# Small VectorE operations, a table built on TensorE instead of by transfers, a later square root and a tail in four parts: one change to a two-branch sequence kernel

## The chip, the cores and the metric

One core of one Trainium2 chip. The span, which the profile's views use, runs from the first to the last instruction and is some 1.8 us shorter than the time.

## The reference, cut to what matters

The input is 2048 tokens of 640 channels. Four residual layers follow one another, A, B, A, B, each behind a layer norm:

```python
x = x + _A_ref(_layernorm(x), Lambda, B, C, log_dt, Dskip)   # complex linear recurrence over the tokens
x = x + _B_ref(_layernorm(x), k, v, shift_k, ssm_k, ssm_D)   # q * (long convolution of k_shift*v + ...)
x = x + _A_ref(...)                                          # the same weights again
x = x + _B_ref(...)

# in _A_ref, per channel p of 640:
Lam_bar = exp(dt * Lam);  B_bar = ((Lam_bar - 1) / Lam)[:, None] * Bmat     # the factor here is "f"
h = Lam_bar * h + B_bar u_t;  y_t = 2 Re(C h) + x * Dskip
# in _B_ref, which does not depend on x except through q:
Y = irfft(rfft(kv, 2S) * rfft(ssm_k, 2S))[:S] + kv * ssm_D;  return q * Y
```

## The kernel before

Every piece of work is a task with a name, an engine, buffers and a wished time; a list scheduler puts the tasks into one order per engine when the kernel is built. Engines execute their own list strictly in that order. So a change of one task's cost or place shifts hundreds of others, and a diff of the code shows less than half of what changes.

The names that matter: `kv_` is the product k_shift*v (five blocks of 128 channels; its `ds` are diagonals that GpSimd builds), `yq0` to `yq4` are the five passes that compute Y (KA, KB and VA, VB transform forward, `pw` multiplies, IB and IA transform back), `a_` are the tables and weights of the A layers, `A1c0` is layer A the first time on chunk 0 of four, and `B2c3` the last B layer on the last chunk. An ending `m` or `mm` is TensorE's part, `e` or `ev` the evacuation of a PSUM tile by ScalarE or VectorE. There are four PSUM tiles of 1024 columns, and TensorE waits when none is free.

The inverse tables of the Y passes are DMA transposes of the forward ones:

```python
for a, b in (("Ci", "Cf"), ("Si", "Sf")):
    def e_tr(_, a=a, b=b):
        nc.sync.dma_start_transpose(out=T[a].get()[:], in_=T[b].get().rearrange("p q k -> p (q k)"))
    t_tr.append(S.add(f"yt_{a}", "sp", 3.5, sins, e_tr, xt=3.5, uses=[T[a], T[b]]))
```

The factor f is 25 operations on 128x5 elements (cut to its first lines):

```python
v.tensor_tensor(den[:], lre, lre, ALU.mult)
v.tensor_tensor(t2[:], lim, lim, ALU.mult)
v.tensor_tensor(den[:], den[:], t2[:], ALU.add)
nc.vector.reciprocal(inv[:], den[:])
# ... 21 more
```

The sine block of ScalarE fills the phase table of layer A, and the roots of the first layer norm (`A1c*_ln_sd`) have no tie to it:

```python
nc.scalar.activation(aw["tab"][:, 2], st["r"], ACT.Sin, scale=-2.0 * PI_LO)
nc.scalar.activation(ab, st["r"], ACT.Abs)
nc.scalar.activation(aw["tab"][:, 1], ab, ACT.Sin, bias=consts["half_pi"][:, 0:1], scale=-2.0 * PI_LO)
for j in range(NJ):
    nc.scalar.activation(aw["rtab"][:, j, :], st["it"], ACT.Identity, scale=0.0, bias=st["r2"][:, j:j + 1])
```

In the last chunk each quarter q takes two fused operations on VectorE, (x - mean) * Y and then times rstd plus x, and two stores follow.

Of the kernel before, what the change touches and what calls it, by code (L numbers as in the profile page):

```python
# [9 lines left out]
ALU = mybir.AluOpType  # L10
# [7 lines left out]
P = 128  # L18
L = 2048
D = 640  # L20
# [32 lines left out]
    "warm": -5, "yt_io0": 2.55, "yt_ph0": 4.27, "yt_sin0": 5.89, "yt_neg0": 9.88, "yt_io6": 132.6, "yt_ph6": 8.2, "yt_sin6": 9.91, "yt_neg6": 13.01,  # L53
    "yt_io12": 8.8, "yt_ph12": 11.54, "yt_sin12": 13.59, "yt_neg12": 16.53, "yt_Ci": 21.14, "yt_Si": 22.8, "yt_nsi": 30.27, "yt_f0": 1.22, "yt_f2": 6.07,
    "yt_f3": 8.4, "yt_f4": 9.65, "yt_h0": 0.07, "yt_h1": 0.97, "yt_h2": 5.13, "yt_h3": 9.63, "kv_dsl": 1.97, "kv_kd": 2.73, "kv_k0": 13.36, "kv_k1":
    14.32, "kv_k2": 14.97, "kv_d0": 5.67, "kv_d1": 6.57, "kv_d2": 10.23, "kv_ds0": 10.65, "kv_lk0": -0, "kv_lv0": 9.8, "kv_mm0:0": 12.25, "kv_ev0:0":
    15.4, "kv_mm0:1": 15.02, "kv_ev0:1": 17.2, "kv_st0": 21.1, "kv_ds1": 13.44, "kv_lk1": 12.55, "kv_lv1": 15, "kv_mm1:0": 21.79, "kv_ev1:0": 25.02,
    "kv_mm1:1": 20.06, "kv_ev1:1": 22.17, "kv_st1": 32.7, "kv_ds2": 18.01, "kv_lk2": 35.6, "kv_lv2": 40.3, "kv_mm2:0": 48.16, "kv_ev2:0": 52.03,
    "kv_mm2:1": 40.92, "kv_ev2:1": 50.79, "kv_st2": 54.8, "kv_ds3": 30.92, "kv_lk3": 47.3, "kv_lv3": 43.8, "kv_mm3:0": 54.17, "kv_ev3:0": 56.25,
    "kv_mm3:1": 57.88, "kv_ev3:1": 59.99, "kv_st3": 76.1, "kv_ds4": 55.32, "kv_lk4": 68.7, "kv_lv4": 72.6, "kv_mm4:0": 78.97, "kv_ev4:0": 81.57,  # L60
    "kv_mm4:1": 72.36, "kv_ev4:1": 77.61, "kv_st4": 85.5, "a_pl": 0.17, "a_p0": 11.24, "a_p1": 13.98, "a_p2": 14.63, "a_p3": 15.78, "a_p4": 18.43, "a_p5":
    20.56, "a_p6": 23.36, "a_lamd": 23.86, "a_f": 28.37, "a_dd": 16.07, "a_ldB0": 2.4, "a_ldB1": 7.4, "a_wl00:0": 34.4, "a_wl00:1": 31.5, "a_wc00:0":
    37.93, "a_wm00:0": 39.1, "a_wc00:1": 40.53, "a_wm00:1": 40.04, "a_wl01:0": 40.21, "a_wl01:1": 37.9, "a_wc01:0": 42.58, "a_wm01:0": 49.98, "a_wc01:1":
    51.1, "a_wm01:1": 53.25, "a_wl02:0": 46.1, "a_wl02:1": 42.6, "a_wc02:0": 48.69, "a_wm02:0": 54.03, "a_wc02:1": 55.37, "a_wm02:1": 58.88, "a_wl03:0":
    71.4, "a_wl03:1": 56.5, "a_wc03:0": 74.94, "a_wm03:0": 75.97, "a_wc03:1": 76.97, "a_wm03:1": 79.87, "a_wl04:0": 65.2, "a_wl04:1": 74.9, "a_wc04:0":
    78.59, "a_wm04:0": 80.65, "a_wc04:1": 81.65, "a_wm04:1": 82.89, "a_b00:0": 9.82, "a_b0e0:0": (10.51, 0), "a_b00:1": 8.06, "a_b0e0:1": (9.33, 3),
    "a_b00:2": 11.53, "a_b0e0:2": (13.01, 1.5), "a_b00:3": 10.63, "a_b0e0:3": (12.42, -1), "a_b00:4": 7.7, "a_b0e0:4": (8.75, 3), "a_b01:0": 49.89,
    "a_b0e1:0": (50.52, 3), "a_b01:1": 14.62, "a_b0e1:1": (17.28, 0.8), "a_b01:2": 23.8, "a_b0e1:2": (24.94, 3), "a_b01:3": 18.33, "a_b0e1:3": (19.59,
    -1), "a_b01:4": 23.52, "a_b0e1:4": (24.36, 1.5), "a_b10:0": 33.92, "a_b1e0:0": (35, 3), "a_b10:1": 32.55, "a_b1e0:1": (33.68, 0), "a_b10:2": 25.31,
    "a_b1e0:2": (26.42, -1), "a_b10:3": 29.77, "a_b1e0:3": (31.02, 0), "a_b10:4": 26.8, "a_b1e0:4": (28.17, 3), "a_b11:0": 42.65, "a_b1e1:0": (43.58, -1),  # L70
    "a_b11:1": 28.31, "a_b1e1:1": (29.65, -1), "a_b11:2": 34.63, "a_b1e1:2": (35.54, -1), "a_b11:3": 46.77, "a_b1e1:3": (48.11, 99), "a_b11:4": 30.56,
    "a_b1e1:4": (31.47, -1), "a_gm0": 84.5, "a_ge0": (87.86, -1), "a_gm1": 87.84, "a_ge1": 90.96, "a_gm2": 104.18, "a_ge2": (107.4, 0), "a_gm3": 98.47,
    "a_ge3": (115.43, 1.5), "a_gm4": 92.78, "a_ge4": 96.07, "a_wl10:0": 97.9, "a_wl10:1": 89.8, "a_wc10:0": 115.48, "a_wm10:0": 107.45, "a_wc10:1":
    111.58, "a_wm10:1": 112.92, "a_wl11:0": 101.84, "a_wl11:1": 103.04, "a_wc11:0": 106.68, "a_wm11:0": 109.36, "a_wc11:1": 121.12, "a_wm11:1": 122.95,
    "a_wl12:0": 116.24, "a_wl12:1": 117.44, "a_wc12:0": 121.91, "a_wm12:0": 132.45, "a_wc12:1": 135.94, "a_wm12:1": 138.06, "a_wl13:0": 131.59,
    "a_wl13:1": 130.39, "a_wc13:0": 137.56, "a_wm13:0": 138.85, "a_wc13:1": 139.99, "a_wm13:1": 141.05, "a_wl14:0": 144.12, "a_wl14:1": 142.92,
    "a_wc14:0": 148.92, "a_wm14:0": 150.68, "a_wc14:1": 153.82, "a_wm14:1": 157.45, "a_ti": 20.17, "a_ta": 22.96, "a_t0": 26.17, "a_t1": 122.82, "a_t2":
    131.25, "yq0_kl": 4.8, "yq0_ka": 15.17, "yq0_KA:m0": 16.75, "yq0_KA:e0": (18.76, -1), "yq0_KA:m1": 19.31, "yq0_KA:e1": 20.32, "yq0_KA:m2": 17.03,
    "yq0_KA:e2": (17.86, -1), "yq0_KA:m3": 18.61, "yq0_KA:e3": (19.66, 99), "yq0_KB:m0": 25.89, "yq0_KB:e0": (27.01, 99), "yq0_KB:m1": 27.38, "yq0_KB:e1":
    (28.75, 0.8), "yq0_KB:m2": 24.08, "yq0_KB:e2": (25.52, 1.5), "yq0_KB:m3": 28.87, "yq0_KB:e3": (30.31, 0), "yq0_KB:m4": 26.57, "yq0_KB:e4": 27.91,  # L80
    "yq0_vl": 26.3, "yq0_VA:m0": 31.92, "yq0_VA:e0": (32.55, 0), "yq0_VA:m1": 31.61, "yq0_VA:e1": (32.24, 6), "yq0_VA:m2": 32.27, "yq0_VA:e2": (33.15,
    0.8), "yq0_VA:m3": 33.47, "yq0_VA:e3": (34.1, 99), "yq0_VB:m0": 35.91, "yq0_VB:e0": 36.98, "yq0_VB:m1": 37.48, "yq0_VB:e1": (38.73, 99), "yq0_VB:m2":
    36.58, "yq0_VB:e2": (37.97, 0), "yq0_VB:m3": 38.79, "yq0_VB:e3": (41.58, 0), "yq0_VB:m4": 40.18, "yq0_VB:e4": (39.51, 1.5), "yq1_kl": 28.99, "yq1_ka":
    34.59, "yq1_KA:m0": 39.9, "yq1_KA:e0": (41.76, 1.5), "yq1_KA:m1": 35.29, "yq1_KA:e1": (35.98, 6), "yq1_KA:m2": 35.57, "yq1_KA:e2": 36.58, "yq1_KA:m3":
    38.6, "yq1_KA:e3": (39.71, 0.8), "yq1_KB:m0": 43.29, "yq1_KB:e0": (44.32, 3), "yq1_KB:m1": 45.76, "yq1_KB:e1": (47.02, 0), "yq1_KB:m2": 44.86,
    "yq1_KB:e2": 46.12, "yq1_KB:m3": 43.97, "yq1_KB:e3": 45.22, "yq1_KB:m4": 47.51, "yq1_KB:e4": 49.78, "yq0_pw": 42.46, "yq0_IB:m0": 52.34, "yq0_IB:e0":
    53.78, "yq0_IB:m1": 51.44, "yq0_IB:e1": (52.78, 99), "yq0_IB:m2": 50.27, "yq0_IB:e2": (51.82, 0), "yq0_IB:m3": 53.95, "yq0_IB:e3": (54.47, 3),
    "yq0_IB:m4": 53.05, "yq0_IB:e4": 54.88, "yq0_tt": 64.47, "yq1_vl": 49.69, "yq1_VA:m0": 56, "yq1_VA:e0": (56.63, -1), "yq1_VA:m1": 57.69, "yq1_VA:e1":
    (58.43, 3), "yq1_VA:m2": 56.43, "yq1_VA:e2": (57.53, 3), "yq1_VA:m3": 56.75, "yq1_VA:e3": (57.6, -1), "yq1_VB:m0": 59.7, "yq1_VB:e0": 60.79,
    "yq1_VB:m1": 61.49, "yq1_VB:e1": (62.75, 0.8), "yq1_VB:m2": 60.37, "yq1_VB:e2": (61.69, 0.8), "yq1_VB:m3": 62.39, "yq1_VB:e3": 63.65, "yq1_VB:m4":  # L90
    61.27, "yq1_VB:e4": (62.15, -1), "yq0_IA:m0": 65.54, "yq0_IA:e0": (66.37, 6), "yq0_IA:m1": 66.03, "yq0_IA:e1": (67.27, 0.8), "yq0_st": 69.05,
    "yq2_kl": 52.2, "yq2_ka": 58.65, "yq2_KA:m0": 64.22, "yq2_KA:e0": (65.38, -1), "yq2_KA:m1": 63.55, "yq2_KA:e1": (64.19, -1), "yq2_KA:m2": 64.8,
    "yq2_KA:e2": (65.43, -1), "yq2_KA:m3": 63.86, "yq2_KA:e3": (64.49, 6), "yq2_KB:m0": 68.05, "yq2_KB:e0": (69.33, 99), "yq2_KB:m1": 66.86, "yq2_KB:e1":
    (68.17, 1.5), "yq2_KB:m2": 68.73, "yq2_KB:e2": (70.23, 0.8), "yq2_KB:m3": 69.62, "yq2_KB:e3": (71.13, 1.5), "yq2_KB:m4": 67.83, "yq2_KB:e4": (69.07,
    1.5), "yq1_pw": 66.59, "yq1_IB:m0": 78.02, "yq1_IB:e0": (79.4, -1), "yq1_IB:m1": 74.47, "yq1_IB:e1": (75.77, 0), "yq1_IB:m2": 76.21, "yq1_IB:e2":
    (77.78, 0.8), "yq1_IB:m3": 77.12, "yq1_IB:e3": (78.82, -1), "yq1_IB:m4": 75.54, "yq1_IB:e4": (76.67, 3), "yq1_tt": 80.49, "yq2_vl": 64.11,
    "yq2_VA:m0": 74.09, "yq2_VA:e0": (74.72, 0), "yq2_VA:m1": 71.61, "yq2_VA:e1": 72.94, "yq2_VA:m2": 71.25, "yq2_VA:e2": (73.84, 3), "yq2_VA:m3": 70.96,
# [312 lines left out]
def a_setup_tasks(S, nc, wp, St, consts, t_go, A_Lambda_re, A_Lambda_im, A_B_re, A_B_im, A_C_re, A_C_im, A_log_dt, A_Dskip, after_sin):  # L410
# [240 lines left out]
    def e_t2(_):  # L651
# [5 lines left out]
        v.tensor_scalar(aw["ctab"][:, 2, :], st["sn"][:, 1, :], -1.0, None, ALU.mult)  # L657

    T["tab"] = [S.add("a_t2", "dve", 1.2, [t_t1], e_t2)]

    T["w"] = w0s + w1s + gs
    return aw, T, t

# [879 lines left out]
```

## Time and profile before

| | before |
|---|---|
| time, median of 3 | 358.37 us (358.19 to 359.01) |
| span of the profiled execution | 356.8 us |
| TensorE's last matmul ends | 345.70 us |
| VectorE's last operation ends | 353.60 us |
| TensorE's gaps over 60 ns, 8 to 40 us / 40 to 142 us / after 142 us | 7.8 / 6.8 / 0 us |
| stretches at half clock before TensorE's end | one, 36.8 to 40.3 us |

TensorE's first real matmuls (columns: start, length, engine, line, operation, count, and in brackets the idle time before it and what ended that):

```profile
9.65 1.01 PE L572 MATMUL ps<-ident_bf,tab 128*128 128x128 bf16 x15 [1.05 <-DMA tab<-in_A_B_re_dram]
...
13.20 0.39 PE L1163 MATMUL ps<-b,fd 128*128 128x512 bf16 x1 [1.28 <-POOL fd L1141]
14.28 1.61 PE L1163 MATMUL ps<-b,fd 128*128 128x512 bf16 x6 [0.69 <-POOL fd L1141]
```

TensorE waits here for diagonals (`fd`) that GpSimd builds one after another, in two pieces of 1.28 and 0.69 us.

### The profile page before, as it was taken

The page shows a single profiled execution, that of the slowest core. Times are in us where ns is not written, and L with a number is a line of the kernel's source. Part 1 is how long each engine was busy: PE and PEld are TensorE (multiplying, and loading weights), DVE is VectorE, ACT ScalarE, POOL GpSimd, SP SyncE. Part 2 cuts the span into 40 slices and gives each one's busy share as a digit, 9 for nine tenths or more (in the row PEclk, how much of TensorE's full clock was granted, in tenths as well). Part 3 has the DMA queues.
Part 4 walks back from the last instruction along what each step waited for, and adds up shares of the span by engine and source line. Part 5 has one row for each costly group of instructions (what it writes and reads, how often), then busy time and mean ns, then how long its engine had stood idle before and what let it go on. Part 6 is the DMA issues. An engine that isn't in the chain of part 4 may idle for free.

```text
span 356.8 us, 8409 instructions
## 1 busy us (share of the span) xinstructions
PE 327.5 (92%) x3534; PEld 247.6 (69%) x3565; DVE 315.1 (88%) x479; ACT 256.4 (72%) x406; POOL 20.8 (6%) x51
## 2 busy tenths in 40 slices
PE   7686998989998997999999999999999999999970
PEld 7346876867686986986685677686866767755640
DVE  8799798798799797999999969979999679999896
ACT  3999798898799999943378599797256577306850
POOL 5841003000000000000000000000000000000000
PEclk9999899999999999999999999999999999999996
DMA  7999999999999982790226690605032022220141
GB/s 193 208 235 188 182 184 217 193 186 202 237 245 163 184 174 46 144 233 2 62 73 119 137 333 34 147 18 132 0 68 81 3 16 59 75 75 2 50 172 73
DMA packets 118712, 45.91 MB, mean 129 GB/s; under 512 B 111629, under 2 KB 112914, under 8 KB 118674
## 3 DMA queue, kind: packets, MB, share of 16 engines
q1 hardware_dynamic: 118528, 45.36, 59.9%
q8 instruction: 28, 0.46, 0.5%
q14 instruction: 10, 0.08, 0.1%
q10 hardware_dynamic: 146, 0.01, 0.0%
HBM read 17.38 MB, written 7.86 MB: 71 GB/s over the span
## 4 chain that ended last, share of the span: by engine, by line
PE 69%; ACT 10%; DVE 8%; DMA 7%; issue 3%; SPq 2%; DVEq 0%; ACTq 0%
PE ps L859 31%; PE ps L770 11%; PE ps L773 11%; ACT b L382 6%; PE ps L608 3%; PE ps L1163 3%; DMA b<-in_A_C_im_dram 2%; DMA b<-in_B_v_dram 2%; DVE b L1169 2%; PE ps L1313 2%; DMA b<-b 2%; PE ps L1314 1%; PE ps L1208 1%; SPq L536 1%; DMA b<-in_B_k_dram 1%
## 5 line engine op out<-in xcount | busy, mean ns | idle before, releaser
L382 ACT ACTIVATE b<-ps 128x1024 bf16<-128x1024 f32 (+3 forms) x125 | 109.6, 945 | 29.5 <-PE ps L773 25.5
L859 PEld LDWEIGHTS <-b 128*128 128x128 bf16 x880 | 67.7, 98 | 48.3
L859 PE MATMUL ps<-W,b 128*128 128x128 bf16 (+1 forms) x629 | 95.7, 298 | 0.6
L770 PE MATMUL ps<-b,BT 128*128 128x256 bf16 x400 | 56.8, 273 | 0.0
L773 PE MATMUL ps<-b,BT 128*128 128x256 bf16 x400 | 56.7, 273 | 0.0
L808 DVE TENSOR_TENSOR_SCAN b<-rtab,b 128x1290 bf16<-128x1290 f32 x16 | 44.7, 2833 | 0.3
L773 PEld LDWEIGHTS <-BT 128*128 128x128 bf16 x400 | 39.1, 98 | 4.5
L770 PEld LDWEIGHTS <-BT 128*128 128x128 bf16 x400 | 38.6, 98 | 4.4
L726 ACT ACTIVATE b<-b,nmr,rstd 128x640 bf16<-128x640 f32 (+1 forms) x43 | 37.0, 915 | 6.2 <-DVE nmr L693 6.2
L681 ACT ACTIVATE junk<-b,nmean 128x640 bf16<-128x640 f32 x48 | 39.7, 828 | 1.5
L1232 PE MATMUL ps<-b,b 128*128 128x128 bf16 x170 | 35.1, 219 | 1.2 <-ACT G L382 0.7
L1235 PE MATMUL ps<-b,b 128*128 128x128 bf16 x170 | 35.4, 219 | 0.0
L1237 PE MATMUL ps<-b,b 128*128 128x128 bf16 x150 | 32.8, 219 | 0.0
L1234 PE MATMUL ps<-b,b 128*128 128x128 bf16 x150 | 32.8, 219 | 0.0
L384 DVE CAST b<-ps 128x1024 bf16<-128x1024 f32 (+2 forms) x24 | 26.2, 1109 | 6.3 <-PE ps L1208 2.7
L867 ACT ACTIVATE b<-ps 128x640 f32<-128x640 f32 x16 | 11.1, 697 | 22.8 <-PE ps L859 22.8
L859 PE MATMUL ps<-G,b 128*128 128x128 bf16 (+1 forms) x152 | 26.5, 295 | 0.4
L1163 PE MATMUL ps<-b,fd 128*128 128x512 bf16 x73 | 18.6, 380 | 3.8 <-POOL fd L1141 2.0
L1313 PE MATMUL ps<-b,b 128*128 128x128 bf16 x160 | 19.4, 219 | 2.6 <-ACT b L382 2.1
L1314 PE MATMUL ps<-b,b 128*128 128x128 bf16 x160 | 19.2, 219 | 0.0
L552 ACT ACTIVATE b<-b,s_F 128x640 f32<-128x640 bf16 x20 | 17.2, 859 | 1.8 <-DVE W L556 1.4
L556 DVE SCALAR_TENSOR_TENSOR W<-b,s_F 128x640 bf16<-128x640 bf16 x20 | 17.4, 882 | 1.0 <-ACT b L552 0.7
(210 smaller groups left out, 560.3 us busy)
## 6 DMA issues: line engine op xcount, KB each, us to landing
b<-in_A_x_dram SPq DMA_DIRECT2D x8, 640.0 KB, 4.9
b<-ysd SPq DMA_DIRECT2D x8, 640.0 KB, 5.1
b<-in_B_ssm_k_dram SPq DMA_DIRECT2D x5, 512.0 KB, 8.6
kvd<-b SPq DMA_DIRECT2D x5, 512.0 KB, 4.3
b<-kvd SPq DMA_DIRECT2D x5, 512.0 KB, 5.4
ysd<-b SPq DMA_DIRECT2D x5, 512.0 KB, 5.0
out_dram<-b SPq DMA_DIRECT2D x8, 320.0 KB, 2.2
tab<-in_A_B_re_dram SPq DMA_DIRECT2D x1, 800.0 KB, 7.4
```

The source lines that it names most:

```text
L382: nc.scalar.activation(out, in_, ACT.Copy)
L681: nc.scalar.activation(small.junk, src(q), ACT.Square, bias=st["nmean"][:, i:i + 1], scale=1.0, accum_out=st["ssq"][:, i:i + 1])
L726: nc.scalar.activation(dst, src, ACT.Identity, bias=st["nmr"][:, i:i + 1], scale=st["rstd"][:, i:i + 1])
L770: nc.tensor.matmul(pb[:, jj, c2, :], lhsT=aw["BT1"][:, c2, j, k, :], rhs=uT[:, 0:2, k, :], start=(k == 0), stop=False)
L773: nc.tensor.matmul(pb[:, jj, c2, :], lhsT=aw["BT0"][:, c2, k, j * P:(j + 1) * P], rhs=uT[:, 2:4, k, :], start=False, stop=(k == NJ - 1))
L808: nc.vector.tensor_tensor_scan(gv, rt, gv, 0.0, ALU.mult, ALU.add)
L859: nc.tensor.matmul(pc[:, o0:o1], lhsT=lh, rhs=rh, start=(n == 0), stop=(n == len(ops) - 1))
L1163: nc.tensor.matmul(pk[:, 512 * b:512 * (b + 1)], lhsT=s_ds.get()[:, l, :], rhs=kT[:, t0:t0 + 512], start=(l == 0), stop=(l == 3))
L1232: nc.tensor.matmul(ps[:, g, 0, :], lhsT=T["Cf"].get()[:, q, :], rhs=are, start=True, stop=single)
L1234: nc.tensor.matmul(ps[:, g, 0, :], lhsT=T["Sf"].get()[:, q, :], rhs=A[:, 2 * q + 1, :], start=False, stop=True)
L1235: nc.tensor.matmul(ps[:, g, 1, :], lhsT=T["NSf"].get()[:, q, :], rhs=are, start=True, stop=single)
L1237: nc.tensor.matmul(ps[:, g, 1, :], lhsT=T["Cf"].get()[:, q, :], rhs=A[:, 2 * q + 1, :], start=False, stop=True)
```

## The change

The intent: fewer small operations on VectorE, two transposes fewer in a DMA queue that is full up to 120 us, two table loads fewer on ScalarE, and a tail that is spread over three engines. The core of the diff (cut; the table of wished times, some 130 lines, is new throughout):

```diff
-        den, t2, inv = tl("den", [P, NJ]), tl("t2", [P, NJ]), tl("inv", [P, NJ])
-        v.tensor_tensor(den[:], lre, lre, ALU.mult)
-        ... 25 operations on 128x5
+        v.tensor_tensor(sq[:], L2, L2, ALU.mult)
+        v.tensor_tensor(den[:], sq[:, 0], sq[:, 1], ALU.add)
+        ... 16 operations, most on 128x10: both parts of a complex number at once
@@ inverse tables
-            nc.sync.dma_start_transpose(out=T[a].get()[:], in_=T[b].get().rearrange("p q k -> p (q k)"))
+        for q0, q1 in ((0, 6), (6, 12), (12, NQ)):
+                for q in range(q0, q1):
+                    nc.tensor.matmul(s_ps.get()[:, (q - q0) * P:(q - q0 + 1) * P], lhsT=T[b].get()[:, q, :], rhs=consts["ident_bf"][:], start=True, stop=True)
+            ... and an evacuation by ScalarE or VectorE for each of the six groups
@@ roots of the first layer norm: behind the sine
-    t_sd = S.add(name + "_sd", "act", ..., [t_bn], e_sd)
+    t_sd = S.add(name + "_sd", "act", ..., [t_bn] + after, e_sd)        # after = AT["t1"], the sine block
@@ last chunk
-            if len(qs) == 1:                  # two fused operations for every quarter
+            if qs[0] == 3:                    # for the last quarter only; the others: ScalarE, product, sum
-                            nc.vector.tensor_tensor(s_Y.get()[:, q, :], b, x, ALU.add)
+                            (nc.gpsimd if eng == "pool" else nc.vector).tensor_tensor(s_Y.get()[:, q, :], b, x, ALU.add)
```

## The prediction

> **What bounds the kernel now.** I read the page first, then the busy times by stretch, then TensorE's waits by stretch, then the order in time of ScalarE, of the transfers and of the last 20 us.
>
> ```profile
> PE 327.5 (92%) x3534; PEld 247.6 (69%) x3565; DVE 315.1 (88%) x479; ACT 256.4 (72%) x406; POOL 20.8 (6%) x51
> PE 69%; ACT 10%; DVE 8%; DMA 7%; issue 3%; SPq 2%; DVEq 0%; ACTq 0%
> ```
>
> TensorE is busy for 92% of the span and carries 69% of the chain that ended last. A busy share can hide stages, so I cut the span where TensorE changes character (columns: stretch, length, then busy us and count of TensorE, its weight loads, VectorE, ScalarE, GpSimd; granted clock, DMA share, GB/s):
>
> ```profile
> 0.00:8.00 8.00, 6.22 (x73) 6.12 (x73) 6.45 (x31) 2.48 (x4) 5.04 (x18) 1.00 0.73 186
> 8.00:40.00 32.00, 24.11 (x302) 17.95 (x305) 26.52 (x72) 29.67 (x45) 12.80 (x27) 0.95 1.06 209
> 40.00:142.00 102.00, 94.57 (x1367) 77.19 (x1372) 86.97 (x123) 94.32 (x118) 2.94 (x6) 1.00 1.00 186
> 142.00:346.00 204.00, 202.65 (x1803) 146.35 (x1820) 187.63 (x245) 128.52 (x237) 0.00 (x0) 1.00 0.35 86
> 346.00:357.00 11.00, 0.00 (x0) 0.00 (x0) 7.49 (x12) 1.42 (x4) 0.00 (x0) 0.72 0.29 114
> ```
>
> From 142 us to 345.7 us TensorE has no idle time that the view of waits lists: a packed stream. So the time can come down in three places only: TensorE's idle time before 142 us, the work that it is given, and the 11 us after its last matmul. The 8 us at the start are matmuls on an identity to wake the clock and the wait for the first matrix.
>
> The view of waits for the first 40 us and for 40 to 142 us, the largest entries (who waits, for whom, us in total, times, longest):
>
> ```profile
> PE ps L1163 <- POOL fd L1141: 2.0, 2, 1.3
> PE ps L1208 <- DVE BT L384: 1.7, 1, 1.7
> PE ps L587 <- DVE b L487: 1.3, 1, 1.3
> ...
> PE ps L1313 <- ACT b L382: 2.1, 1, 2.1
> PE ps L1208 <- ACT b L382: 1.4, 4, 0.5
> ```
>
> Between 8 and 40 us TensorE idles about 7.1 us, between 40 and 142 us 6.6 us (sums of that view; the first leaves out 1.8 us ahead of the first matmul). The 1.7 us wait at 34 us has a tail: right after it the granted clock falls to one half (columns: stretch, length, TensorE busy, clock, DMA):
>
> ```profile
> 37.00:38.00 1.00, 1.00 (x14) 0.50 1.04 221
> 38.00:39.00 1.00, 1.00 (x12) 0.50 1.58 43
> ```
>
> At half clock for some 3.2 us, about 1.6 us of work is lost. So 7.1 + 1.6 + 6.6 = 15.3 us is what reordering could give at most.
>
> **What the Trainium skill says.** "TensorE: Matmul & The Clock Gate", Part 1, gives a start-to-start of 55.6 ns for a warm 128-column matmul, and half rate when the array has been idle over a window of about 3.4 us. The trace agrees on the first (ten of them in a row take 0.56 us in the chain that ended last). On the second it is looser: idle time of 1.7 us, in a stretch that was thin before, was enough here.
> "ScalarE: Activation LUTs", What ACT_TABLE_LOAD costs, gives 1283 ns for a load plus a drain of 1380 ns. The trace shows 1.28 us each, six of them, and no gap of the drain's size around the two below.
> "SBUF — State Buffer", Who interferes with whom, says that a VectorE instruction with two SBUF inputs contends with a GpSimd instruction that reads SBUF, and that the loser blocks. The trace agrees: four 128x128 GpSimd products take 3.41 us at 24.6 us, beside VectorE's 2.31 us diagonal build, against 1.46 us for four in a quieter place.
>
> **The change part by part.**
>
> *f in 16 operations.* Before, 25 operations of 128x5 elements run from 31.12 to 34.34 us, 3.2 us: dependent ones start 0.20 us apart, independent ones 0.08. The new form has 16, some 7 of them dependent: 7 x 0.20 + 9 x 0.09 = 2.2 us. VectorE gains about 1.0 us, and it lies just ahead of the BT copy that TensorE waits 1.7 us for. But the new order builds the diagonals after three evacuations of the power tables, so a part of this is given back.
>
> *Inverse power tables.* Two DMA transposes go:
>
> ```profile
> 19.89 2.42 SPq L987 DMA_TRANSPOSE b<-b  x1
> 23.07 3.75 SPq L987 DMA_TRANSPOSE b<-b  x1
> ```
>
> They land 4.5 and 5.8 us after issue, in a stretch where the DMA share is 1.06; dropping them lets every later load and store start up to some 9 us sooner. In return TensorE gets 34 matmuls of 128 columns: 34 x 56 ns = 1.9 us, all added to the engine that bounds. Six evacuations of 640 or 768 columns are added: three on ScalarE at about 0.72 us, three on VectorE at 0.75 to 0.96 us (the page's 128x768 cast took 958 ns).
>
> *Roots behind the sine.* Before, ScalarE runs Sqrt at 103 us, the sine at 126.6 and Sqrt again at 134.9, each with its table load:
>
> ```profile
> 126.65 1.28 ACT L644 ACT_TABLE_LOAD   x1
> ...
> 131.83 2.11 ACT L648 ACTIVATE rtab<-b,s_r 128x258 f32<-128x258 f32 x5
> ...
> 134.87 1.28 ACT L712 ACT_TABLE_LOAD   x1
> 136.17 0.30 ACT L712 ACTIVATE std<-mv,eps 128x4 f32<-128x4 f32 x1
> ```
>
> In the 9.8 us from 126.65 to 136.47 ScalarE copies one PSUM tile only, and at 135.3 us TensorE stands 2.1 us for a ScalarE copy: the largest wait after 40 us. With every first-layer root after the sine, the sine finds its table still there from the setup, and one load of Sqrt follows: two loads fewer, 2.6 us. The five G products now stand far earlier in TensorE's order, so the sine block comes at the third Y pass, with other work queued for TensorE. I take this 2.1 us as gone.
>
> *The tail, which the short name of the change does not tell.* Before, TensorE's last matmul is over at 345.7 us and VectorE has nearly all of the last chunk still to do:
>
> ```profile
> 345.89 0.81 DVE L871 SCALAR_TENSOR_TENSOR b<-ps,b 128x640 f32<-128x640 f32 x1
> ...
> 348.35 2.47 DVE L901 SCALAR_TENSOR_TENSOR b<-b,nmean,b 128x640 bf16<-128x640 f32 x3
> 350.86 1.68 DVE L905 SCALAR_TENSOR_TENSOR b<-b,rstd,b 128x640 bf16<-128x640 bf16 x2
> ...
> 352.72 0.88 DVE L905 SCALAR_TENSOR_TENSOR b<-b,rstd,b 128x640 bf16<-128x640 bf16 x1
> ```
>
> Eight operations of 0.81 us net (0.88 less the overlap) end at 353.6 us, 7.9 us after TensorE. In the new order three quarters of the chunk have their normalising step on ScalarE, a product of 640 elements on VectorE (a quarter of the 2560-element one of 1.49 us, about 0.43 us), and two of the final sums (and two of the chunk before) on GpSimd. After TensorE's end VectorE then has: residual 0.85, three products 1.3, one sum 0.8, reciprocal pair 0.35, two fused operations 1.75: 5.1 us. GpSimd's two sums of 640 elements were never run here; five times the 0.36 us of a 128-element one is 1.8 us, an estimate, and each can block VectorE's two-input operations. I add 0.9 us: 6.0 us in place of 7.9. Four stores in place of two change little; from the last issue to the end stays 3.2 us.
>
> **The sum**, at the end of the span: table matmuls +1.9; idle time from 40 to 142 us from 6.6 to 2.7, -3.9 (2.1 the sine, 1.8 from earlier transfers); idle and half clock from 8 to 40 us from 8.7 to 7.2, -1.5 (the tables wait for all sines, which now come later, so TensorE's early order is not free of holes); tail -1.9. Together -5.4 us: 358.4 - 5.4 = 353.0 us, 1.5% faster.
>
> **The rivals.**
> *VectorE becomes the bound.* It has 315 us of work and was idle some 35 us before the second layer's last reconstruction. Adding up the measured durations in each kernel's own order, the new order puts about 5 us more on VectorE ahead of the third Y product and about 11 us more ahead of that last reconstruction, since it moves residual sums there. If VectorE then keeps the idle time it has now, TensorE must wait in the first layer, where VectorE is 97% busy already, and the gain is eaten: 357 to 360 us. For it: those sums. Against: VectorE's idle time before 142 us is nearly all waiting for TensorE and ScalarE, and shrinks when the queue is fuller.
> *The transfers were the bound up to 120 us.* Their share is at 1.0 and above there. Then 9 us less transfer pulls the whole setup forward, the idle time between 8 and 142 us nearly vanishes and the half-clock dip with it: -10 us or more, 346 to 348 us. Against: in the view of waits a DMA is named as TensorE's last releaser for 1.1 us only.
> *The tail collides.* GpSimd and VectorE block each other in the last 8 us and the last store slips by 1 to 3 us: 354 to 356 us.
>
> **Range and chances.** The middle is 353.0. The first and third rivals reach to about 357, the second to 347: 8 in 10 between 347.5 and 357.0. Over 2% faster means below 351.2, which needs some 2 us beyond my sum; 0.33. Within 2%, 0.64. Over 2% slower would need VectorE to bound and new holes in the packed stretch; 0.03.
>
> **What would show it.** Right: two table loads fewer on ScalarE, no wait of 2 us on a ScalarE copy around the Y passes, TensorE's last matmul at 341 to 344 us, and 5 to 7 us from there to VectorE's last operation. Wrong: TensorE idle in many small pieces after 142 us, released by VectorE (first rival); idle time under 5 us in all between 8 and 142 us (second rival: I was too careful); GpSimd sums of over 2.5 us or VectorE products of over 0.6 us after TensorE's end (third rival). If the half-clock dip remains, or a second one appears, my -1.5 is lost.

## More of the kernel before

The metric is device time in microseconds (us), the median of several executions.

(In sums of TensorE's gaps over 60 ns, gaps of some 50 ns, the distance of two 128-column products, are left out: a record of the trace may be missing there.)

## The result, and the profile after

The changed kernel is correct and takes 361.68 us (360.76 to 362.08, four runs) against 358.51 us for the kernel before in the same rounds: a ratio of 1.0084, 95% interval 1.0059 to 1.0108. All ratios here are the mean time of one kernel's fast runs over that of the kernel before in the same rounds, so not quite the ratio of the medians. 3.0 us slower where 5.4 us faster were predicted, and outside the range.

The page of the kernel after, busy times and the chain that ended last:

```profile
PE 332.8 (93%) x3599; PEld 250.5 (70%) x3599; DVE 322.3 (90%) x478; ACT 249.6 (70%) x401; POOL 25.2 (7%) x55
PE 75%; DVE 11%; ACT 9%; DMA 2%; issue 2%; POOL 0%; SPq 0%; DVEq 0%; POOLq 0%; ACTq 0%
```

Transfers left the chain (7% before, 2% now), and TensorE's share of it rose from 69% to 75%. The transfers were relieved, and no time came back. The table by stretch (columns as in the prediction):

```profile
8.00:40.00 32.00, 24.70 (x250) 16.38 (x248) 28.18 (x64) 27.25 (x43) 13.56 (x33) 0.94 1.04 205
40.00:142.00 102.00, 94.91 (x1435) 78.44 (x1434) 90.87 (x121) 94.38 (x122) 0.11 (x1) 0.99 0.89 174
142.00:346.00 204.00, 204.00 (x1818) 147.73 (x1816) 187.37 (x247) 121.99 (x226) 0.94 (x1) 1.00 0.36 86
```

From 40 to 142 us the DMA share fell from 1.00 to 0.89, VectorE gained 3.9 us of work and TensorE is busy as long as before: its idle time has not shrunk. (Its 34 new products lie ahead of this stretch, at 21 to 27 us.) The view of waits for TensorE, the first 40 us and then 40 to 142 us:

```profile
PE ps L1174 <- POOL fd L1152: 2.1, 1, 2.1
PE ps L1243 <- DVE b L1180: 1.9, 1, 1.9
...
PE ps L1219 <- ACT b L385: 2.5, 7, 0.5
PE ps L1243 <- ACT b L385: 2.0, 4, 0.7
PE ps L1324 <- DVE G L387: 0.9, 1, 0.9
```

The wait of 2.1 us for a ScalarE copy is gone, as predicted. In its place stand fifteen waits of up to 0.7 us for ScalarE's copies and one of 0.9 us for VectorE's. The waits for ScalarE add up to 5.6 us in this stretch, as much as before the change. And the two early waits of 1.28 and 0.69 us for GpSimd's diagonals have become one of 2.06 us. Sums of TensorE's gaps over 60 ns: 7.3 us from 8 to 40 us (7.8 before), 7.0 us from 40 to 142 us (6.8 before), none later, in both kernels.

A wait can cost twice: for the wait itself, and when the clock halves behind it. The table by microsecond for the kernel after (the third number from the end is the granted clock; TensorE's busy time is full in these rows because it works slowly, not because it does much):

```profile
12.00:13.00 1.00, 0.06 (x1) 0.06 (x1) 0.97 (x5) 1.00 (x2) 0.92 (x3) 0.59 0.25 48
13.00:14.00 1.00, 1.00 (x3) 0.25 (x3) 0.00 (x0) 1.00 (x2) 1.00 (x4) 0.50 1.28 287
14.00:15.00 1.00, 1.00 (x3) 0.40 (x3) 0.00 (x0) 1.00 (x2) 1.00 (x4) 0.50 1.26 284
...
40.00:41.00 1.00, 1.00 (x12) 1.00 (x11) 0.61 (x1) 1.00 (x2) 0.00 (x0) 0.50 0.65 140
41.00:42.00 1.00, 1.00 (x17) 0.80 (x15) 0.00 (x0) 1.00 (x3) 0.00 (x0) 0.50 1.57 199
```

In its profiled execution the kernel after has two stretches of 3.4 us at half clock before TensorE's end (12.2 to 15.6 and 39.5 to 42.9 us), one at each of the two long early waits; the kernel before has one. Such a stretch costs at most half its length, 1.7 us.

One execution each doesn't make this a property of the kernels, however. A stretch that begins between 11 and 16 us is in all ten kept traces with the early GpSimd order of the kernel after, but also in five of the eight with that of the kernel before. Over whole executions the mean granted clock was 0.974 to 0.989 in the 55 runs of the kernel before that the experiments list, and 0.980 to 0.983 in the four of the kernel after; the mean is 0.982 for both. The profiled execution of the kernel before, at 0.987, was one of the better ones. Nor must one more stretch make TensorE end later: the run b_tail below has the order of the kernel before up to the last chunk, and two such stretches, but its gaps from 8 to 40 us are 6.7 us in place of 7.8, and TensorE ends at 345.10 us in place of 345.70.

The sine block now lies where TensorE fills tile after tile. ScalarE, then VectorE beside it, kernel after:

```profile
105.38 1.28 ACT L636 ACTIVATE tab<-b 128x1290 bf16<-128x1290 f32 x1 [0.62 <-PE ps L600]
106.57 1.26 ACT L637 ACTIVATE rtab<-b 128x1290 f32<-128x1290 f32 x1
107.86 1.37 ACT L638 ACTIVATE tab<-rtab,half_pi 128x1290 bf16<-128x1290 f32 x1
109.27 2.11 ACT L640 ACTIVATE rtab<-b,s_r 128x258 f32<-128x258 f32 x5
111.38 1.28 ACT L705 ACT_TABLE_LOAD   x1
112.68 0.30 ACT L705 ACTIVATE std<-mv,eps 128x4 f32<-128x4 f32 x1
```

```profile
107.69 0.82 DVE L387 CAST G<-ps 128x640 bf16<-128x640 f32 x1
108.42 4.61 DVE L387 CAST b<-ps 128x1024 bf16<-128x1024 f32 x4
```

For 7.6 us ScalarE copies nothing; from 107.7 us on VectorE alone empties the tiles, 1.13 us from start to start, while TensorE fills a tile in 1.05 us. The table loads fell from six to four, as predicted, at no gain to the end.

The tail, from TensorE's last matmul (it ends at 348.97 us) on, GpSimd and VectorE of the kernel after:

```profile
349.80 2.49 DVE L916 TENSOR_TENSOR b<-b,b 128x640 bf16<-128x640 bf16 x3
...
350.50 3.05 POOL L924 TENSOR_TENSOR b<-b,b 128x640 bf16<-128x640 bf16 x2 [1.39 <-ACT nmean L669]
...
352.33 1.91 DVE L924 TENSOR_TENSOR b<-b,b 128x640 bf16<-128x640 bf16 x1
```

Three products that take 0.48 us each when undisturbed take 2.49 us here: the third stretches to 1.68 us beside GpSimd's two sums, and a sum of 0.82 us to 1.91 us, 2.3 us in all. Still VectorE ends 7.25 us after TensorE instead of 7.90, and the span ends 2.8 us after that instead of 3.2: the tail gained 1.05 us.

So in the two profiled executions: TensorE's end +3.3 us, the tail -1.05 us, the span +2.2 us.

### The profile page after: what moved, and what is told of

Read it like the earlier page. It is cut to its first block, busy times and chain, and to the rows that moved or that the text cites. A ratio compares the mean times of both kernels' runs of the same rounds, so it can differ in the third digit from the quotient of the medians.

```text
span 359.0 us, 8522 instructions
## 1 busy us (share of the span) xinstructions
PE 332.8 (93%) x3599; PEld 250.5 (70%) x3599; DVE 322.3 (90%) x478; ACT 249.6 (70%) x401; POOL 25.2 (7%) x55
## 4 chain that ended last, share of the span: by engine, by line
PE 75%; DVE 11%; ACT 9%; DMA 2%; issue 2%; POOL 0%; SPq 0%; DVEq 0%; POOLq 0%; ACTq 0%
PE ps L852 32%; PE ps L763 12%; PE ps L766 12%; ACT b L385 7%; PE ps L1174 3%; PE ps L600 2%; DVE b L387 2%; DMA b<-in_A_C_re_dram 2%; PE ps L1324 2%; PE ps L1325 2%; PE ps L1219 2%; PE ps L1243 1%; PE ps L1246 1%; PE ps L1248 1%; PE ps L1245 1%
## 5 line engine op out<-in xcount | busy, mean ns | idle before, releaser
L385 ACT ACTIVATE b<-ps 128x1024 bf16<-128x1024 f32 (+3 forms) x123 | 105.7, 942 | 23.6 <-PE ps L766 21.9
L387 DVE CAST b<-ps 128x1024 bf16<-128x1024 f32 (+3 forms) x32 | 34.8, 1104 | 8.4 <-PE ps L1248 3.3
L719 ACT ACTIVATE b<-b,nmr,rstd 128x640 bf16<-128x640 f32 (+1 forms) x40 | 34.7, 914 | 5.1 <-DVE nmr L686 4.2
L924 POOL TENSOR_TENSOR b<-b,b 128x640 bf16<-128x640 bf16 x4 | 7.1, 1796 | 294.6 <-DVE b L916 293.2
L852 PE MATMUL ps<-G,b 128*128 128x512 bf16 (+1 forms) x160 | 27.0, 299 | 0.0
L1174 PE MATMUL ps<-b,fd 128*128 128x512 bf16 x80 | 19.6, 399 | 2.5 <-POOL fd L1152 2.1
```

The source lines that it names most:

```text
L385: nc.scalar.activation(out, in_, ACT.Copy)
L387: nc.vector.tensor_copy(out, in_)
L719: nc.scalar.activation(dst, src, ACT.Identity, bias=st["nmr"][:, i:i + 1], scale=st["rstd"][:, i:i + 1])
L852: nc.tensor.matmul(pc[:, o0:o1], lhsT=lh, rhs=rh, start=(n == 0), stop=(n == len(ops) - 1))
```

## The experiments

**How they were made.** If one part is taken out of the diff, the list scheduler gives a new order and everything moves. For each experiment I therefore wrote the order and the buffers of one of the two kernels down as a fixed list and edited only the tasks named. With no edit, these fixed lists give the two kernels back instruction for instruction. Each was run in five rounds against the kernel before; "+x us against the kernel after" is the difference to its ratio of 1.0084, times 358 us.

| run | base | edit | median us | ratio (95%) |
|---|---|---|---|---|
| b_f16 | before | f in 16 operations | 357.74 | 0.9989 (0.9960 to 1.0018) |
| b_pe_tab | before | tables on TensorE | 363.56 | 1.0162 (1.0135 to 1.0189) |
| b_no_tab | before | no table transposes | 358.23 | 0.9988 (0.9962 to 1.0015) |
| b_no_sine | before | no sine block | 356.21 | 0.9934 (0.9907 to 0.9960) |
| b_f_late | before | f later | 360.95 | 1.0089 (1.0068 to 1.0111) |
| b_ds_first | before | diagonals earlier | 358.53 | 1.0008 (0.9984 to 1.0032) |
| b_tail | before | new tail, no GpSimd | 356.67 | 0.9962 (0.9942 to 0.9981) |
| b_tail_f16 | before | b_tail and b_f16 | 355.12 | 0.9916 (0.9901 to 0.9931) |
| a_dma_tab | after | tables by transposes | 366.36 | 1.0239 (1.0209 to 1.0269) |
| a_no_tab | after | no inverse tables | 361.13 | 1.0066 (1.0036 to 1.0096) |
| a_sine_late | after | sine block late | 374.74 | 1.0476 (1.0441 to 1.0511) |
| a_no_sine | after | no sine block (spoiled) | 362.69 | 1.0122 (1.0089 to 1.0156) |
| a_no_sine2 | after | no sine block | 361.04 | 1.0092 (1.0070 to 1.0115) |
| a_no_sine3 | after | the same, evacuations shared | 359.72 | 1.0043 (1.0029 to 1.0058) |
| a_f_first | after | small work behind an evacuation | 361.37 | 1.0102 (1.0081 to 1.0124) |
| a_early | after | GpSimd's early order | 358.75 | 1.0043 (1.0004 to 1.0082) |
| a_tail_dve | after | all sums on VectorE | 360.92 | 1.0088 (1.0066 to 1.0110) |
| a_tail_dve2 | after | the last two sums on VectorE | 360.73 | 1.0083 (1.0054 to 1.0112) |

The theory I began with: TensorE's idle time before 142 us was not removed but moved, because it is set by the order of the setup and by four PSUM tiles, not by the amount of work in any one part; the 34 products came on top. The rivals were the prediction's own: the parts give what was predicted and something else (VectorE, the tail) eats it, or the transfers had been the bound.

### f alone

```diff
 order of the kernel before, unchanged
-    a_f: 25 operations
+    a_f: 16 operations
```

> The kernel before, its order of instructions written down and kept, with f in 16 operations alone. Before, the 25 took 3.22 us on VectorE; in the changed kernel the 16 took 2.85 us. Theory (f is worth almost nothing): 16 operations at 2.8 to 2.9 us, total within 0.6 us of before (357.8 to 358.8). Rival (my prediction: 1.0 us off VectorE just ahead of the wait at 34 us, and with it the half-clock dip): 2.2 us and a total 1 to 2.5 us faster.

357.74 us, ratio 0.9989: nothing by itself. But the trace shows the part that was predicted: the 16 operations take 2.31 us (31.71 to 34.02) in place of 3.22, and the wait behind them 0.8 us in place of 1.7. In the kernel after the same 16 take 2.85 us. The reason stands on GpSimd's line. VectorE (an excerpt) and GpSimd, kernel after:

```profile
35.25 0.37 DVE L506 TENSOR_SCALAR s_w<-s_lam 128x5 f32<-128x5 f32 x1
...
35.73 0.25 DVE L508 TENSOR_TENSOR s_sq<-s_w,s_pf 128x10 f32<-128x10 f32 x1
...
36.39 0.33 DVE L511 TENSOR_TENSOR s_fg<-s_sq,s_den 128x10 f32<-128x10 f32 x1
```

```profile
35.18 1.51 POOL L1152 TENSOR_TENSOR fd<-ident_bf,skf 128x128 bf16<-128x128 bf16 x4 [12.21 <-PE ps L1174]
```

The same lines in the run b_f16, where GpSimd is idle:

```profile
32.25 0.16 DVE L416 TENSOR_SCALAR s_w<-s_lam 128x5 f32<-128x5 f32 x1
...
32.52 0.17 DVE L418 TENSOR_TENSOR s_sq<-s_w,s_pf 128x10 f32<-128x10 f32 x1
...
33.01 0.17 DVE L421 TENSOR_TENSOR s_fg<-s_sq,s_den 128x10 f32<-128x10 f32 x1
```

What follows: the new order put f beside four GpSimd products, and 0.54 of the 0.91 us that f gained went to operations stretched beside them. This is read from the overlap in time; no run took the GpSimd products away.

### The tables: by transposes or on TensorE, in either order

```diff
 b_pe_tab: order of the kernel before, tasks yt_Ci, yt_Si (transposes) removed
+    six groups of products and six evacuations, between 25 and 38 us; yt_nsi two evacuations later
 a_dma_tab: order of the kernel after, the six groups and evacuations removed
+    yt_Ci, yt_Si (transposes) behind the second store of kv; yt_nsi (VectorE) later
```

> The kernel before, order kept, with the inverse tables as TensorE products alone (34 matmuls and six evacuations put into TensorE's thin stretch from 25 to 32 us; the two DMA transposes gone). Theory (TensorE's and the evacuating engines' work is what counts, the transfers were hidden): slower by 1 to 4 us, 359.5 to 362.5. Rival (the transfers bound the setup, two fewer pull it forward): faster by 3 us or more, under 355.5.

> The changed kernel, order kept, with the two DMA transposes back in place of the 34 matmuls and six evacuations. Theory (hidden transfers, paid work): faster than the changed kernel by 2 to 4 us, 357.7 to 359.7. Rival (transfers bound): slower than it by 3 us or more, over 364.5.

363.56 us (ratio 1.0162, +5.8 us against the kernel before) and 366.36 us (1.0239, +5.6 us against the kernel after). Both are worse than the kernel they were made from, b_pe_tab by more than the 1 to 4 us that my theory gave: each order fits its own form of the table. Each form was tried in one place only, and the small operation behind the table (`yt_nsi`) had to move with it, so this does not show which form is cheaper as such. In b_pe_tab TensorE's gaps from 25 to 45 us rise from 2.9 to 4.9 us, and it is at half clock from 11.4 to 18.2 and 31.8 to 35.3 us, 10 us in place of 3.4. In a_dma_tab the loads stand behind the transposes in the queue, and TensorE waits for one of them:

```profile
35.84 1.45 PE L1075 MATMUL ps<-b,fd 128*128 128x512 bf16 x3 [4.70 <-DMA b<-in_B_k_dram]
```

For a_dma_tab my theory expected a gain of 2 to 4 us, and the rival, that the transfers matter, held: but only for the order after, which asks for these loads some 13 us sooner (the third K load is issued at 23 us instead of 36).

### The tables taken away

```diff
 b_no_tab, a_no_tab: the inverse passes read the forward tables
-    transposes (b_no_tab); 34 products and six evacuations (a_no_tab)
```

> The kernel before without its two table transposes, result wrong on purpose: the relief of the transfers by itself, at no price to TensorE. The prediction's step (earlier transfers are worth 1.8 us of TensorE's idle time, and some of the early holes): 1.5 to 3.5 us shorter than the kernel before, ratio 0.990 to 0.996. Theory now (in an order fitted to them the transposes were hidden): within 0.7 us, ratio 0.998 to 1.002.

> The kernel after without its inverse tables: no 34 products, no six evacuations; the inverse passes read the forward tables, so the result is wrong on purpose. Theory (the 34 products are paid in full, their evacuations add to waits): 2 to 4 us shorter than the kernel after, ratio to the kernel before 0.997 to 1.003. Rival (they fill holes that TensorE has anyway): within 1 us of the kernel after, ratio 1.005 to 1.011.

(Both results are wrong. The comparison with the reference evidently does not feel this branch, so "correct" says nothing about these tables.)

b_no_tab: 0.9988, nothing. This is the relief of the transfers at no price: the third K load, for one, is issued at 31.5 us instead of 35.9. Against it stand the prediction's 1.8 us for earlier transfers (the interval allows 1.4 us at most), and the second rival with them. The order of the other engines is fixed here, though, so this is shown for the old order alone. a_no_tab: 1.0066, 0.6 us less than the kernel after, and the intervals overlap: taking 1.9 us of TensorE's work and some 5 us of evacuations away gives nearly nothing back. In its profile TensorE's time before 142 us is eaten by new waits and by the clock: half rate from 11.7 to 18.5 and from 28.7 to 32.1 us. My theory of this run (2 to 4 us) fell, its rival held. So TensorE's added work is not by itself the price in this order; that the order of the setup is the price is argued, not shown.

### The sine block: moved, and taken away

```diff
 a_sine_late: order of the kernel after
-    ... a_t1 (sine block) at 105 us, first two roots, ...
+    ... first two roots, ... a_t1 before the first evacuation of layer A (142 us)
 b_no_sine, a_no_sine, a_no_sine2: ScalarE does nothing in a_t1; GpSimd fills the table with a constant
 a_no_sine3: as a_no_sine2, and
-    a_ge0, yq3_KB:e3, yq3_KB:e2 on VectorE
+    a_ge0, yq3_KB:e3, yq3_KB:e2 on ScalarE
```

> The changed kernel, order kept but for the sine block, which goes behind the first two layer-one roots again, to where TensorE makes the first projection of layer one (11 us of matmuls with few evacuations). Two table loads come back, 2.6 us of ScalarE. Theory (the block of 7.5 us at 105 us leaves VectorE alone to evacuate at 1.2 us a tile, and TensorE falls behind by 3 to 4 us there): the many waits from 105 to 125 us shrink, total faster than the changed kernel by 1.5 to 4 us, 357.7 to 360.2. Rival (two loads fewer are a gain): slower than the changed kernel by 1 us or more, over 362.7.

374.74 us, far outside what either theory said. By the profile there are two causes: the sine's buffer is held 37 us longer, and loads and Y passes wait for it (my reading, not tested); and the block falls between evacuations again, at 150 us, where TensorE then stands 7.3 us:

```profile
PE ps L1236 <- ACT b L297: 7.3, 1, 7.3
PE ps L1131 <- ACT b L297: 6.3, 9, 2.7
```

It does not tell what the sine costs in the kernel after, but it explains why the change put it early.

> The kernel before without the same block, result wrong on purpose. The prediction's step (2.1 us of TensorE's idle time are the sine's): 1.5 to 3 us shorter than the kernel before, ratio 0.9915 to 0.996. Rival (the wait at 135 us is taken up by later slack, or another wait takes its place): within 0.7 us, ratio 0.998 to 1.002.

> The kernel after without ScalarE's sine block (two sines, an absolute value, five broadcasts; GpSimd fills the table with a constant long before), result wrong on purpose. Theory (in its new place, among dense evacuations, the block costs TensorE about what it cost in the old place, in many small waits): 1.5 to 3.5 us shorter than the kernel after, ratio 0.998 to 1.004. Rival (the prediction's step: the block costs nothing there): within 0.7 us of the kernel after, ratio 1.006 to 1.0105.

> As the run a_no_sine, with GpSimd's constant fill moved behind its last other work of the setup (at 52 us), so that it delays no load; result wrong on purpose. Theory (the sine block, in its new place, still costs TensorE what it cost in the old one): 1.5 to 3.5 us shorter than the kernel after, ratio to the kernel before 0.998 to 1.004. Rival (the step of the prediction was right and the block costs nothing in the new place, so that the loss lies elsewhere): within 0.7 us of the kernel after, ratio 1.006 to 1.0105.

> The kernel after without the sine block, as a_no_sine2, and with three of the evacuations that VectorE did while ScalarE was at the sine given to ScalarE, which stood idle for 5.5 us in a_no_sine2; result wrong on purpose. Theory (the block's cost in the new place is that VectorE must evacuate alone, one tile in 1.13 us, where TensorE fills one in 0.9 to 1.05): TensorE's waits at 108 to 118 us go, 1.0 to 2.5 us shorter than a_no_sine2, ratio to the kernel before 1.001 to 1.0065. Rival (TensorE is held there by something else): within 0.6 us of a_no_sine2, ratio 1.0075 to 1.011.

On the kernel before the block costs 2.4 us (ratio 0.9934): the prediction's 2.1 us was right, the rival fell. On the kernel after the first try was spoiled, by the fill. GpSimd, VectorE and TensorE in a_no_sine:

```profile
37.95 2.25 POOL L547 MEMSET tab<- 128x2580 bf16 x1
...
38.55 1.72 DVE L427 TENSOR_SCALAR s_F<-s_fg 128x10 f32<-128x10 f32 x1
...
40.25 0.23 PE L491 MATMUL ps<-b,tab 128*128 128x128 bf16 x1 [2.70 <-POOL b L1069]
```

The fill writes into the buffer `tab`, in which the matrix in_A_B_re still lay at that time. TensorE's next product on this matrix therefore waited 2.70 us for GpSimd, and then read what the fill had written. Beside the fill, VectorE's operation on 128x10 elements, 0.17 us when undisturbed, took 1.72 us and ended with it. (I took the hole for a delayed load; the trace shows this instead.) With the fill moved behind the setup, where it stretches nothing (VectorE's six products beside it take 7.67 us, as elsewhere), a_no_sine2 gave 1.0092, no gain at all, which looked like the prediction's step being right: the block costs nothing in its new place. The trace of a_no_sine2 says otherwise. ScalarE, without its sine:

```profile
105.43 1.28 ACT L616 ACT_TABLE_LOAD   x1
106.72 0.30 ACT L616 ACTIVATE std<-mv,eps 128x4 f32<-128x4 f32 x1
112.55 1.02 ACT L297 ACTIVATE b<-ps 128x1024 bf16<-128x1024 f32 x1 [5.53 <-DVE b L299]
```

ScalarE stood idle for 5.5 us, and VectorE went on emptying the tiles alone, because the fixed list says which engine evacuates what. The experiment had taken away the cause and kept its consequence. By stretch, from 105 to 118 us, VectorE's 12.93 us of 13 (the third pair) show who bounds there:

```profile
105.00:118.00 13.00, 11.03 (x191) 9.66 (x189) 12.93 (x23) 7.23 (x11) 0.00 (x0) 1.00 0.35 76
```

a_no_sine3 gives three of these evacuations to ScalarE: 1.0043, 1.5 us less than the kernel after and 1.8 us less than a_no_sine2, with intervals that do not overlap. The wait of 0.9 us on VectorE is gone from its view of waits. So in the new place the block still costs about 1.5 us, through VectorE, where it cost 2.4 us in the old place, through ScalarE. Of the predicted 2.1 us some 0.9 us are left as a gain; each of the two effects has an interval of about 1 us either way, so this rest is not told from nothing.

### The early holes

```diff
 b_f_late (before), VectorE
-    a_f, yt_nsi, a_b1e0:3, yq0_VA:e0, a_b1e0:1
+    a_b1e0:3, yq0_VA:e0, a_f, yt_nsi, a_b1e0:1
 a_f_first (after), VectorE
-    a_t0, yt_nsi, a_f, kv_ev2:1, kv_ev2:0
+    a_f, kv_ev2:1, kv_ev2:0, a_t0, yt_nsi
```

> The kernel before with nothing changed but the place of the small operations on f and of the negation of the sine table: both behind the first evacuation of the first Y pass, so that the evacuation TensorE waits 1.7 us for at 34 us comes 3 us sooner. Theory (TensorE's early holes are set by the place of small VectorE work, not by its amount): the 1.7 us wait and the half-clock window behind it go, 2 to 3.3 us shorter than the kernel before, ratio 0.991 to 0.995. Rival (the hole is set by something else, ScalarE or a transfer, and moves elsewhere as it did in the changed kernel): within 0.7 us, ratio 0.998 to 1.002.

> The kernel after with two small VectorE pieces (first angle step and the negation of the sine table) moved behind the evacuation that TensorE waits 1.9 us for at 37 us. Theory, same as for the kernel before: that wait falls below 1 us and its half-clock window may go, 1 to 3 us shorter than the kernel after, ratio 1.000 to 1.006. Rival: the hole moves, ratio 1.007 to 1.010.

Both miss. b_f_late is 3.2 us slower: the 1.7 us wait is gone and one of 3.4 us stands a little later, since f and the table's sign now lie ahead of the small sum (`yq1_ka`) that the next Y pass starts from, and TensorE runs at half clock from 39.3 to 46.2 us:

```profile
PE ps L1121 <- DVE b L1172: 3.4, 1, 3.4
```

In a_f_first the wait of 1.9 us is gone, its gaps from 25 to 45 us grow from 4.0 to 4.6 us and the half-clock stretch stays (43.9 to 47.3 us). In both places that were tried, the evacuation behind some 3 us of small work is late. Whether less of that work would help more than another place for it is not shown: f in 16 operations alone took nothing off the time (b_f16).

```diff
 a_early (after), GpSimd; VectorE's yt_ph12 follows the ramp
-    yt_io6, ..., yt_f4, kv_ds0, kv_ds1, yt_io12, a_dd
+    yt_io6, yt_io12, ..., kv_ds0, kv_ds1, yt_f4, a_dd
 b_ds_first (before), GpSimd
-    yt_f4, kv_ds0, kv_ds1
+    kv_ds0, yt_f4, kv_ds1
```

> The kernel after with the early order of GpSimd changed, and nothing else: the small table of the Y transform comes behind the first two groups of diagonals instead of ahead of them (2.2 us), and the third index ramp comes before the diagonals (so VectorE's 3.1 us of idle time at 13 us and ScalarE's 1.4 us go). Theory (the wait of 2.1 us on GpSimd at 11 us and the half-clock window that follows it in every run of the changed kernel are a loss of the new order, which the kernel before has in half its runs only): 1.5 to 4 us shorter than the kernel after, ratio 0.998 to 1.004. Rival (the hole moves on to the next wait): within 0.7 us, ratio 1.006 to 1.0105.

> The kernel before with the small table of the Y transform behind the first group of diagonals on GpSimd: the wait on GpSimd at 12 us shrinks by 1.3 to 2 us. Theory: 0.7 to 2.5 us shorter than the kernel before, ratio 0.993 to 0.998. Rival (the hole moves on): within 0.5 us, 0.9985 to 1.0015.

a_early: 358.75 us, ratio 1.0043, 1.5 us less than the kernel after, just outside the expectation. Its runs spread from 357.8 to 362.7 us, so its interval touches that of the kernel after: likely, not proven. The one profiled execution agrees with the reason given. TensorE, run a_early:

```profile
11.22 0.29 PE L1035 MATMUL ps<-ident_f,b 80*128 80x80 f32 x1 [0.46 <-ACT BT L297]
11.44 0.23 PE L364 MATMUL ps<-ident_f,b 20*128 20x20 f32 x1
11.74 5.57 PE L1086 MATMUL ps<-b,fd 128*128 128x512 bf16 x25
```

The products of kv start at 11.74 instead of 12.95 us without a wait, there is no half clock before 40 us in this execution, and TensorE ends at 346.50 instead of 348.97 us. A like cure on the kernel before, with one group of diagonals moved, gives nothing (1.0008); its waits there were two short ones already, which may be why.

### The tail

```diff
 a_tail_dve, a_tail_dve2 (after)
-    B2c2_m:2, B2c2_m:3, B2c30_m:0, B2c31_m:1 on GpSimd
+    all four on VectorE (a_tail_dve); the last two on VectorE (a_tail_dve2)
 b_tail (before): three quarters of the last chunk
-    two fused operations of 0.88 us on VectorE
+    normalising on ScalarE, product (0.48 us) and sum (0.82 us) on VectorE; a store per quarter
 b_tail_f16 (before): b_tail and the 16 operations of b_f16
```

> The kernel after with its four GpSimd sums of 640 elements (two of the chunk before last, two of the last chunk) given to VectorE, order otherwise unchanged. Theory (GpSimd and VectorE block each other after TensorE's end: VectorE's operations were stretched by 2.3 us, and the four sums cost VectorE some 0.8 us each, of which two lie after TensorE's end): 0.3 to 1.5 us shorter than the kernel after, ratio to the kernel before 1.004 to 1.008. Rival (GpSimd takes a real load off the tail): 1 to 3 us longer than the kernel after, ratio 1.011 to 1.017.

> As the run before it, but only the last chunk's two sums go from GpSimd to VectorE; the two of the chunk before last stay. Theory of blocking: those two stayed beside evacuations that TensorE's last matmuls wait for, so this run shows which pair costs; 0 to 1 us shorter than the kernel after if the last pair carries it, ratio 1.006 to 1.0085. Rival: 1 us longer, ratio 1.011.

> The kernel before with the new form of the tail alone, and no GpSimd in it: three quarters of the last chunk normalised on ScalarE, then a product and a sum on VectorE in place of two fused operations; four stores in place of two. From the durations: three quarters at 0.48 + 0.82 us less overlap in place of 2 x 0.88, and a smaller last store. Theory: 1.3 to 2.3 us shorter than the kernel before, ratio 0.9935 to 0.9965. Rival (last operations wait for ScalarE's normalising or the stores queue up): within 0.7 us, 0.998 to 1.002.

> The kernel before with the new form of the tail, without GpSimd, and f in 16 operations: the two parts of the change that did not lose when run alone. If they add up: 0.9962 times 0.9989 is 0.995, 356.3 to 356.8 us. If f's form only moves a hole: as b_tail, 0.996 to 0.9975.

a_tail_dve and a_tail_dve2 are not told apart from the kernel after (1.0088, 1.0083): of the contention seen in the trace nothing could be gained, since the sums cost VectorE about what blocking costs it (VectorE ends 6.75 us after TensorE in place of 7.25, in one execution each, and the time does not move). b_tail is 1.4 us faster than the kernel before (0.9962), as expected, and VectorE ends 6.53 us after TensorE in place of 7.90. VectorE in b_tail, two of the operations that replace the fused ones:

```profile
346.03 0.48 DVE L837 TENSOR_TENSOR b<-b,b 128x640 bf16<-128x640 bf16 x1
...
346.55 0.82 DVE L845 TENSOR_TENSOR b<-b,b 128x640 bf16<-128x640 bf16 x1
```

b_tail_f16 is the version that beats both: 355.12 us, ratio 0.9916, 3.0 us faster than the kernel before and correct (four runs, where the other experiments have six). That is more than the two parts alone (0.4 and 1.4 us), but their intervals do not exclude a plain sum. Its four runs have a mean granted clock of 0.986 to 0.991, those of b_tail 0.977 to 0.984, and one stretch of 3.4 us at half clock lowers this mean by 0.005; its profile has no half clock at 36 us. The smaller hole behind f cannot be the reason by itself: b_f16 has the same hole, and its runs have 0.978 to 0.987, like the kernel before. Where the surplus comes from stays open.

## Why the prediction was wrong, point by point

The sum of the prediction had four terms. Measured in the two profiled executions:

| term | predicted | measured |
|---|---|---|
| 34 products added | +1.9 | +1.9 in TensorE's busy time; taking them away gives 0.6 |
| idle time, 40 to 142 us | -3.9 | +0.2 |
| idle time, 8 to 40 us, and half clock | -1.5 | -0.6 idle, up to +1.3 at half clock |
| tail | -1.9 | -1.05 |

The measured terms add up to 1.8 us, for a span that grew by 2.2 us; 0.4 us have no name here. So the step that failed is the second and third term: "idle time from 40 to 142 us from 6.6 to 2.7" and "idle and half clock from 8 to 40 us from 8.7 to 7.2". Together they were to give 5.4 us; they cost up to 0.9 us, since TensorE's waits moved to other copies instead of going away. (The 7.1 us behind the 8.7 is a wrong sum, too: the entries of the prediction's own view add up to 7.8 us.)

- *2.1 us for the sine.* The mechanism was right where it was read (2.4 us by b_no_sine), and wrong in "I take this 2.1 us as gone": I looked for other work queued for TensorE at the new place, and TensorE had it, but its tiles had to be emptied by VectorE alone, which is slower than TensorE fills them. About 1.5 us of the cost remained (a_no_sine3).
- *1.8 us from earlier transfers.* Nothing in the old order (b_no_tab, 0.9988). My own reading against the second rival, that a DMA is named as last releaser for 1.1 us only, should have struck this term too.
- *Early holes.* The table's form alone moves 5.6 to 5.8 us in an order made for the other form (b_pe_tab, a_dma_tab). The new order joined two waits for GpSimd into one of 2.06 us; by a_early its early order costs about 1.5 us, likely, not proven. The prediction's warning that a second half-clock dip would lose the -1.5 came true in the profiled execution, but such dips come and go in both kernels, so they are not shown to be what the new kernel lost.
- *f.* 2.2 us predicted, 2.31 us measured in the old order; 2.85 us in the new one, beside GpSimd. That "a part is given back" was said, and the reason given was not it.
- *Tail.* Mis-sized: 1.05 us for 1.9. The contention was predicted at 0.9 us and is 2.3 us of stretched operations.
- *The rivals.* The first came nearest in time (357 to 360 us, still below the 361.68 measured), and its engine was right: VectorE did 12.93 of 13 us at 105 to 118 us. The sign named for it, small idle pieces after 142 us, did not appear; the pieces lie before. The second fell. The third held in the trace but not in the time.

What stays open: the effects measured against the kernel after (0.6, 1.5 and 1.5 us for tables, sine and early order) were not run together, each has an interval of about a microsecond, and they depend on each other through the order. How much of the 3.0 us is due to each part can't be settled by taking one part at a time out of a fixed list; that the idle time moved and did not shrink is shown by the two profiled executions.

## What to carry to other kernels

Before counting a removed wait as a gain, ask which engine must do the displaced work at the new place and whether it is faster than the one that fills its buffers. An experiment that removes a cost but keeps the order that was made around it can show no gain where there is one (a_no_sine2 against a_no_sine3): look in the trace for an engine that now stands idle. And take a large change apart: here two of its parts alone, the tail without GpSimd and the shorter f, gave 3.0 us on the old order, where the whole cost 3.0 us.

## What the Trainium skill lacked or had wrong

- "TensorE: Matmul & The Clock Gate" (Part 1) has the clock fall after an idle window of about 3.4 us. Here the window need not be idle throughout: in the 3.4 us before half clock began at 12.2 us in the kernel after, TensorE was busy for 44% of the time, and before every such stretch of the kept traces (up to TensorE's end) for 2 to 58%. The length of a wait alone does not decide: 1.28 and 0.69 us in the kernel before brought no half clock, 1.34 and 0.69 us at the same place in b_f16 did, at 13.9 us. The stretches last 3.4 us or twice that, as the page's window does.
- "SBUF — State Buffer" (Who interferes with whom) has the rule but hardly any sizes: two GpSimd sums of 128x640 bf16 (1.44 and 1.65 us) stretched a VectorE product from 0.48 to 1.68 us and a sum from 0.82 to 1.91 us; four GpSimd products of 128x128 in 1.51 us stretched VectorE operations of 0.16 or 0.17 us to 0.25 to 0.37 us; and a GpSimd fill of 128x2580 bf16 held a 128x10 `tensor_scalar` for 1.72 us in place of 0.17.
- "ScalarE: Activation LUTs" (What ACT_TABLE_LOAD costs) gives a drain of 1380 ns beside the load of 1283 ns; the load at 111.38 us follows the block before it without a gap, takes 1.28 us, and the root starts at 112.68 us.
- No page that I read says what an experiment with a fixed order can't show; the numbers are 1.0092 against 1.0043 for the same part removed.
